# Four stores issued by ScalarE in y steps 4 and 5 in place of SyncE in step 3, a load put behind the y products, and eight operand tiles moved by 32 words

## The chip, the core and the metric

One core of a Trainium2 chip. A kernel is timed in device microseconds for one execution; the kernel before took 1453.03 us (median of 3 runs, 1451.39 to 1453.51).

Engines: PE is TensorE (matmuls; PEld is its loading of the stationary operand), DVE VectorE, ACT ScalarE, POOL GpSimd, SP SyncE. Each works through its own instructions in the order of the program. SP issues the kernel's DMAs; SPq in the profile is its instruction queue. Engines wait for each other, and for DMAs, by semaphores.

## What is computed

Two layers, each of a Fourier mixing block A and a shift MLP block B, on x of 2048 rows by 512:

```python
def _A_ref(x, dft_seq_re, dft_seq_im, dft_hid_re, dft_hid_im):
    a = jnp.einsum("bsd,ed->bse", x, dft_hid_re)
    b = jnp.einsum("bsd,ed->bse", x, dft_hid_im)
    y = jnp.einsum("ts,bse->bte", dft_seq_re, a) - jnp.einsum("ts,bse->bte", dft_seq_im, b)
    return y

x = x + _A_ref(_layernorm(x))
x = x + _B_ref(_layernorm(x))      # B: layernorm, w1, gelu, shifts by 1 and 2 rows, w2, layernorm, w3, gelu, w4
x = x + _A_ref(_layernorm(x))
x = x + _B_ref(_layernorm(x))
```

Block A takes nearly all that is spoken of here. Block B begins with z, the normed result of A, in turned form (features on the partitions).

## The kernel before

**Products.** Every fp32 number is split in a high and a low part of the type fp32r, and a product is three matmuls (`mm3`, lines 307 to 309): high by high, high by low, low by high. Each matmul has a stationary operand of 128x128 and a moving operand of 128x512. `mm_half` makes two such products, six matmuls.

**Block A by chunks.** The 2048 rows of the result are four chunks c of 512. For each chunk `x_phase` runs eight steps k with the stationary operands `ax[k]`, then `y_phase` eight steps k with `ay[k]`; the moving operand of both is a piece of the sequence matrix, which comes from HBM (`in_ws`). The first chunk of layer 0 has `plain_phase` in place of both. So there are seven x phases and seven y phases. A y step has two items, "by1" and "by0", each of 12 matmuls; `y_order` gives the items in the order 0 by1, 0 by0, 1 by1, ... 5 by0, 6 by1, 7 by1, 6 by0, 7 by0. They are counted 0 to 15 here: items 8 and 9 are step 4, items 10 and 11 step 5, item 12 is 6 by1 and item 13 is 7 by1. An x step has 18 matmuls. After the last chunk's y phase, four "hid" products (96 matmuls, tiles `ring`, `rr`) multiply by the hidden matrix (`in_hs`), and then block B starts (`by_pairs`) with `zt[0]`, the first chunk's turned z, as a moving operand.

**How a moving operand is made.** Each y step needs two pieces of 512 KB. SP loads them into two of four buffers `raw0` to `raw3` (line 235): even steps use raw0 and raw1, odd steps raw2 and raw3. For each item DVE subtracts the pieces (line 259: `ring0f<-raw`), ACT casts the difference to the high part (line 260), DVE makes the low part (line 270: `ring<-ring0f`). There are four `ring` slots; item n uses slot n modulo 4. `stream` works three items ahead on line 259 and two items ahead on line 270, so DVE's order in a y phase is: line 259 of item n+1, line 270 of item n, line 259 of item n+2, line 270 of item n+1, and so on. A load into a raw buffer waits until DVE has done line 259 of both items that read it.

**The turned z of the first chunk.** In the last chunk's y phase (c = 3) `hook(k)` runs other work at the head of each step's by1 item. In steps 1 and 2 ACT norms the four z tiles of the first chunk (line 661); in steps 2 and 3 DVE turns them into `turn0` (line 605, two in each step). In step 3 `turn_out` stores `turn0` to HBM as four DMAs of 256 KB (line 615, buffer `zd`), and in step 6 `turn_in` loads it back as one DMA of 1 MB into `zt[0]` (line 620, `zt0f`), which lies where `ay[0]` and `ay[1]` were. Both are issued by SP, in one line with the loads of line 235. ACT splits `zt0f` and DVE makes its low part (lines 435 and 438) during the hid products.

**Where the operands lie.** All tiles lie in one arena per partition and are placed by a word number (a word is 4 bytes). `ay[0]` to `ay[3]` lie at words 0, 2048, 24640 and 26688. `ZW` is 4128, the length of `zt[0]`; `ay[4]` to `ay[7]` follow each other from there, each 2048 words, then `ax[0]` and `ax[1]`. `ax[2]` to `ax[7]` lie from word 15424. 2048 and 1536, the lengths of an `ay` and an `ax`, are multiples of 64 words (256 bytes), and so are 24640 and 15424; 4128 is 64 times 64 and 32 over.

Of the kernel before, what the change touches and what calls it, by code (L numbers as in the profile page):

```python
# [13 lines left out]
P = 128  # L14
S, D, F = 2048, 512, 1376
# [3 lines left out]
NP = NT // 2  # L19
# [4 lines left out]
DH = D // 2  # L24
NF = -(-F // P)
B = 32
NB = P // B
# [3 lines left out]
HALO = 2  # L31
# [13 lines left out]
def spectral_mlp_kernel(ctx: ExitStack, tc: tile.TileContext, x, ws, hs, w1, w2, w34, out, out_t):  # L45
    nc = tc.nc
# [30 lines left out]
    ZW = KD * 2 * SW  # L77
    AX, AY = 3 * 2 * DH, 4 * 2 * DH
    W12, XS = 2 * ZW, 2 * ZW + 8 * 2 * CH
    H3 = XS + NT * D  # L80
# [9 lines left out]
    def at(name, word, *shape, dtype=F32R):  # L90
        return nc.alloc_sbuf_tensor_at(name, [P, *shape], dtype, offset=base + 4 * word).ap()

    def both(name, word, *shape):
        return at(name, word, *shape), at(name + "f", word, *shape, dtype=F32)

    ay_at = [0, AY, H3, H3 + AY] + [ZW + (k - 4) * AY for k in range(4, NP)]
    ay, ayf = zip(*(both(f"ay{k}", word, 4, 2, DH) for k, word in enumerate(ay_at)))
    ax, axf = zip(
        *(both(f"ax{k}", ZW + 4 * AY + k * AX if k < 2 else XS - 2 * D + (k - 2) * AX, 3, 2, DH) for k in range(NP))
    )  # L100
    zt, ztf = zip(*(both(f"zt{i}", i * ZW, KD, 2, SW) for i in range(2)))
    w12 = [at(f"w12{i}", W12 + i * 4 * CH, 2, 2, CH) for i in range(4)]
# [3 lines left out]
    turn0 = at("turn0", EXT, KD, CH, dtype=F32)  # L106
# [42 lines left out]
    def xt(j):  # L149
        return xs[j // 2][:, j % 2]  # L150
# [4 lines left out]
    count = {"mm": 0, "tmp": 0, "turn": 0}  # L155
# [68 lines left out]
    def rows(sb, d, j, n, load):  # L224
        v = d[j * P : (j + n) * P, :].rearrange("(t p) d -> p t d", p=P)
        nc.sync.dma_start(*((sb, v) if load else (v, sb)))
# [127 lines left out]
    def normed_act(o, s, mr):  # L354
        nc.scalar.activation(o, s, AF.Identity, bias=mr[2], scale=mr[1])
# [84 lines left out]
    late = {}  # L440

    def plain_phase(hook):

        for k in range(NP):
            first, last = k == 0, k == NP - 1
            a = {"11": ay[k][:, 2], "22": ay[k][:, 3], "21": mid[k % 4][:, 0], "12": mid[k % 4][:, 1]}
            s = stream()
            hook(2 * k)
            jobs = ((PB, a["21"], s[:, 1]), (PA, a["11"], s[:, 1]), (PC, a["12"], s[:, 0]), (PD, a["22"], s[:, 0]))
            if first:  # L450
                mm_first(jobs[:2])
                mm_first(jobs[2:])
            else:
                for job in jobs:
                    mm_half(*job, False, False)
            s = stream()
            hook(2 * k + 1)
            mm_half(PC, a["11"], s[:, 1], False, last)
            mm_half(PD, a["21"], s[:, 1], False, last)
            mm_half(PB, a["22"], s[:, 0], False, last)  # L460
            mm_half(PA, a["12"], s[:, 0], False, last)
# [17 lines left out]
    def run_late(*names):  # L479
        for i in names:  # L480
            for f in late.pop(i, ()):
                f()
# [120 lines left out]
    def turn_one(t, q, u):  # L603
        v = t.rearrange("p d (a q j) -> p d a q j", a=NB, q=TC)[:, :, :, q]
        nc.vector.transpose(v, blocks_of(u))

    def turn_out(t, to=None):

        if to is None:
            count["turn"] += 1  # L610
            to = zd[count["turn"] % 2]
        z = to.rearrange("(e i) t -> i e t", i=B)
        for b in range(NB):
            v = t[b * B : (b + 1) * B].rearrange("i d (a t) -> i (d a) t", a=NB)
            nc.sync.dma_start(z[:, :, b * P : (b + 1) * P], v)  # L615

    def turn_in(dst, col):

        z = zd[count["turn"] % 2].rearrange("(d p) t -> p d t", p=P)
        nc.sync.dma_start(dst[:, :, 1, col : col + CH], z)  # L620
# [183 lines left out]
    def by_pairs(layer, zs, xin, dst):  # L804
# [3 lines left out]
        for q in range(TC):  # L808
            turn_one(turn2, q, zs[4 + q])
        turn_out(turn2)  # L810
        state["limit"] += 2
        w2p = [stream(), stream()]
# [154 lines left out]
        A(5, norm(10, 11))  # L967
        D(7, turn(sc0, 2, 2, 3))
        A(7, lambda: turn_out(sc0))
        A(9, lambda: turn_in(ztf[0], HALO))  # L970
        A(12, z_highs(0))
# [13 lines left out]
        D(14, turn(sc1, 3, 0, 1))  # L985
        D(15, turn(sc1, 3, 2, 3))
        A(15, lambda: turn_out(sc1), lambda: edges(NC - 1), lambda: left_halo(3))
        A(17, lambda: turn_in(ztf[1], HALO))
        A(21, z_highs(3))
# [547 lines left out]
    for layer in range(LAYERS):  # L1537
# [4 lines left out]
        for c in range(NC):  # L1542
            if layer == 0 and c == 0:
# [58 lines left out]
                def hook(i):  # L1602
                    k, odd = divmod(i, 2)
                    state["limit"] = w_items[layer]
                    if not odd:
                        if k + 1 < NP:
                            xp_norm(k + 1, 3)
                            xp_main(k + 1)
                        if not k:
                            xp_main_lows(1)  # L1610
                    else:
                        if 0 < k < NP - 1:
                            xp_main_lows(k + 1)
                        if k + 2 < NP:
                            xp_stats(k + 2)
                        if k:
                            xp_sums(k - 1)
                            xp_highs(k - 1, False)
                            xp_lows(k - 1, False)
# [32 lines left out]
            def hook(k):  # L1652
                if k == 1 and c:
                    rows(X1, x1d, (c - 1) * TC + 2, 2, False)
                if c == NC - 1:
                    if k == 6:
                        rows(xs[2], x1d, 4, 2, True)
                    if k in (1, 2):
                        for j in (2 * k - 2, 2 * k - 1):
                            zs[j] = tmp[:, j]  # L1660
                            normed_act(zs[j], xt(j), ln2[j])
                    if k in (2, 3):
                        for j in (2 * k - 4, 2 * k - 3):
                            turn_one(turn0, j, zs.pop(j))
                    if k == 3:
                        turn_out(turn0)
                    if k == 6:
                        turn_in(ztf[0], HALO)

            y_phase(c, hook)  # L1670

        tmps[:] = singles
        count["tmp"] = 0
        run_late("im1-")
        run_late("re1+")
        for i, (ri, dp) in enumerate(HORDER):
# [81 lines left out]
```

## Time and profile before

| | us |
|---|---|
| median of 3 runs | 1453.03 |
| the profiled execution's own time | 1454.25 |
| its span, from the first to the last instruction | 1452.3 |
| PE busy | 1433.5 (99%) |
| DVE busy | 1148.7 (79%) |
| ACT busy | 727.1 (50%) |
| mean granted TensorE clock | 0.994 of full |

The span is what the trace covers; the time of an execution holds another 1.95 us around it. A row of the timeline or the chain begins with its start and its length in us; a busy PE is not PE at its peak, since the ends of matmuls are modelled: how fast PE goes is read from the distance between the starts of matmuls.

### The profile page before, as it was taken

How to read it: one execution, taken by the hardware profiler on the slowest of the kernel's cores; microseconds unless marked ns; L12 is line 12 of the kernel's file. 1: busy time of each engine (PE TensorE's matmuls, PEld its weight loads, DVE VectorE, ACT ScalarE, POOL GpSimd, SP SyncE). 2: the span in 40 equal slices, each digit the busy share in tenths (PEclk: the TensorE clock that was granted, in tenths of full speed). 3: DMA queues.
4: the chain of work that ended last, by engine and by line, in shares of the span. 5: the costliest groups of instructions: out<-in, count | busy, mean ns of one | idle time of the engine just before them, and what ended most of it. 6: DMA issues, size and time to landing. Idle time of an engine off the chain costs nothing.

```text
span 1452.3 us, 17275 instructions
## 1 busy us (share of the span) xinstructions
PE 1433.5 (99%) x6258; PEld 1177.6 (81%) x6258; DVE 1148.7 (79%) x1602; ACT 727.1 (50%) x979; POOL 78.7 (5%) x111
## 2 busy tenths in 40 slices
PE   9999999999799999999999999999998999999998
PEld 7888888888688888888888888888886888888887
DVE  7876987987778888667899879879887698637585
ACT  5553454455366755435554544544454666424352
POOL 2100000000001000000000000000000010000000
PEclk9999999999899999999999999999999999999999
DMA  7326655657554858959756466574666559656594
GB/s 248 129 88 203 203 181 194 205 164 261 196 155 119 284 201 311 380 206 340 237 170 203 159 194 209 163 228 166 198 220 220 157 125 338 196 192 248 171 312 148
DMA packets 136813, 302.13 MB, mean 208 GB/s; under 512 B 15372, under 2 KB 61196, under 8 KB 133528
## 3 DMA queue, kind: packets, MB, share of 16 engines
q1 hardware_dynamic: 136728, 301.03, 62.6%
q8 instruction: 49, 0.80, 0.2%
q14 instruction: 36, 0.29, 0.1%
HBM read 246.18 MB, written 54.81 MB: 207 GB/s over the span
## 4 chain that ended last, share of the span: by engine, by line
PE 93%; DVE 4%; DMA 2%; SPq 1%; issue 0%; ACT 0%; POOL 0%; DVEq 0%; ACTq 0%; POOLq 0%
PE psd L307 10%; PE psd L309 10%; PE psd L308 10%; PE psa L307 8%; PE psa L309 8%; PE psa L308 8%; PE psb L308 6%; PE psc L308 6%; PE psc L307 6%; PE psc L309 6%; PE psb L309 6%; PE psb L307 6%; DMA raw<-in_ws 2%; DVE ring L270 1%; SPq L615 0%
## 5 line engine op out<-in xcount | busy, mean ns | idle before, releaser
L253 ACT CAST ring<-raw 128x1024 fp32r<-128x1024 f32 x127 | 133.2, 1052 | 107.8 <-PE psd L309 50.9
L270 DVE TENSOR_TENSOR ring<-raw,ring 128x1024 fp32r<-128x1024 f32 (+1 forms) x128 | 154.6, 1211 | 24.2 <-ACT ring L253 24.1
L307 PE MATMUL psd<-ring,rr 128*128 128x512 f32 x208 | 81.0, 389 | 0.0
L309 PE MATMUL psd<-ring,rr 128*128 128x512 f32 x208 | 81.0, 389 | 0.0
L308 PE MATMUL psd<-ring,rr 128*128 128x512 f32 x208 | 80.9, 389 | 0.0
L260 ACT CAST ring<-ring0f 128x1024 fp32r<-128x1024 f32 x28 | 29.5, 1054 | 70.1 <-DVE ring0f L259 70.1
L308 PE MATMUL psb<-ring,ay 128*128 128x512 f32 x128 | 51.5, 402 | 13.0 <-DVE ring L270 13.0
L347 POOL TENSOR_TENSOR rs<-ve,mhalf 128x4 f32<-128x4 f32 x16 | 28.7, 1795 | 615.5 <-DVE nm L346 615.5
L270 DVE TENSOR_TENSOR ring<-ring1f,ring 128x512 fp32r<-128x512 f32 (+1 forms) x56 | 53.2, 950 | 0.8 <-ACT ring L256 0.8
L309 PE MATMUL psb<-ring,ay 128*128 128x512 f32 x128 | 51.1, 400 | 0.0
L326 POOL TENSOR_TENSOR rs<-ve,mhalf 128x2 f32<-128x2 f32 (+1 forms) x33 | 29.3, 887 | 397.0 <-DVE nb L325 397.0
L307 PE MATMUL psb<-ring,ay 128*128 128x512 f32 x128 | 50.6, 396 | 0.0
L307 PE MATMUL psc<-ring,ay 128*128 128x512 f32 x128 | 50.5, 394 | 0.0
L308 PE MATMUL psc<-ring,ay 128*128 128x512 f32 x128 | 50.4, 394 | 0.0
L307 PE MATMUL psa<-ring,ay 128*128 128x512 f32 x126 | 50.3, 399 | 0.0
L309 PE MATMUL psc<-ring,ay 128*128 128x512 f32 x128 | 50.1, 391 | 0.0
L309 PE MATMUL psa<-ring,ay 128*128 128x512 f32 x126 | 50.1, 397 | 0.0
L308 PE MATMUL psa<-ring,ay 128*128 128x512 f32 x126 | 50.0, 397 | 0.0
L308 PE MATMUL psd<-ring,ay 128*128 128x512 f32 x126 | 49.4, 392 | 0.0
L309 PE MATMUL psd<-ring,ay 128*128 128x512 f32 x126 | 49.4, 392 | 0.0
L307 PE MATMUL psd<-ring,ay 128*128 128x512 f32 x126 | 49.4, 392 | 0.0
L260 ACT CAST ring<-ring1f 128x1024 fp32r<-128x1024 f32 x28 | 29.5, 1055 | 36.9 <-DVE ring1f L259 36.9
(566 smaller groups left out, 4381.0 us busy)
## 6 DMA issues: line engine op xcount, KB each, us to landing
raw<-in_ws SPq DMA_DIRECT2D x183, 512.0 KB, 4.9
raw<-in_hs SPq DMA_DIRECT2D x56, 512.0 KB, 3.6
w3b<-w3d SPq DMA_DIRECT2D x15, 1792.0 KB, 8.6
w4r<-w4a SPq DMA_DIRECT2D x33, 512.0 KB, 6.4
wq<-w4a SPq DMA_DIRECT2D x22, 512.0 KB, 4.9
w3d<-w3b SPq DMA_DIRECT2D x5, 1792.0 KB, 6.7
x1d<-tmp SPq DMA_DIRECT2D x12, 512.0 KB, 5.9
xs<-x1d SPq DMA_DIRECT2D x12, 512.0 KB, 5.1
```

The costliest lines, as they stand in the source:

```text
L253: nc.scalar.copy(dest[:, a:b, 0], r[0][:, a:b])
L260: nc.scalar.copy(dest[:, :, 0], lo)
L270: nc.vector.tensor_tensor(lo[:, i], src[:, i], hi[:, i].bitcast(F32), op=ALU.subtract)
L307: nc.tensor.matmul(o, lh, rh, start=first, stop=False, skip_group_check=onto)
L308: nc.tensor.matmul(o, lh, rl, start=False, stop=False, skip_group_check=onto)
L309: nc.tensor.matmul(o, ll, rh, start=False, stop=last, skip_group_check=onto)
L326: nc.gpsimd.tensor_tensor(rs[:, :n], ve[:, :n], mhalf[:, 0, :n], op=ALU.pow)
L347: nc.gpsimd.tensor_tensor(rs, ve, mhalf[:, :, :2], op=ALU.pow)
```

## The change

```diff
-    ay_at = [0, AY, H3, H3 + AY] + [ZW + (k - 4) * AY for k in range(4, NP)]
+    ay_at = [0, AY, H3, H3 + AY] + [ZW + B + (k - 4) * AY for k in range(4, NP)]
...
-        *(both(f"ax{k}", ZW + 4 * AY + k * AX if k < 2 else XS - 2 * D + (k - 2) * AX, 3, 2, DH) for k in range(NP))
+        *(both(f"ax{k}", ZW + B + 4 * AY + k * AX if k < 2 else XS - 2 * D + (k - 2) * AX, 3, 2, DH) for k in range(NP))
...
-    def turn_out(t, to=None):
+    def turn_out(t, to=None, queue=nc.sync, which=range(NB)):
...
-        for b in range(NB):
+        for b in which:
...
-            nc.sync.dma_start(z[:, :, b * P : (b + 1) * P], v)
+            queue.dma_start(z[:, :, b * P : (b + 1) * P], v)
...
-                    if k == 3:
-                        turn_out(turn0)
-                    if k == 6:
-                        turn_in(ztf[0], HALO)
+                    if k in (4, 5):
+                        turn_out(turn0, queue=nc.scalar, which=range(2 * k - 8, 2 * k - 6))
...
         tmps[:] = singles
         count["tmp"] = 0
+        turn_in(ztf[0], HALO)
         run_late("im1-")
```

`B` is 32 words. `ay[4]` to `ay[7]`, `ax[0]` and `ax[1]` move from word 4128 to word 4160, which is 65 times 64; `ax[1]` then ends where `ax[2]` begins. The four stores are issued by ACT, two at the head of step 4 and two at the head of step 5, and the load of `zt0f` is issued by SP after the y phase. No other DMA moves to another engine. Both layers have the same differences.

On SP, in the last chunk's y phase, the rows around the four stores (raw buffers with their numbers; the first two loads are those of step 5, the last two those of step 6):

```order
 L235 DMA raw2_178<-in_ws 128x1024
 L235 DMA raw3_179<-in_ws 128x1024
-L615 DMA zd1_80<-turn0_150 32x16x128 x4
 L235 DMA raw0_176<-in_ws 128x1024
 L235 DMA raw1_177<-in_ws 128x1024
```

The loads of step 6 stand directly behind those of step 5, with nothing between that waits for the turning.

On SP further on, at the end of the y phase (`in_hs` is the hidden matrix, `in_w1` and `in_w2` weights of block B, `xs` a part of x):

```order
 L235 DMA raw1_177<-in_hs 128x1024
 L226 DMA xs2_143<-x1d_78 128x2x512
-L620 DMA zt0f_133<-zd1_80 128x4x512
 L235 DMA raw2_178<-in_hs 128x1024
 L235 DMA raw3_179<-in_hs 128x1024
 L235 DMA raw0_176<-in_w1 128x1024
 L235 DMA raw1_177<-in_w1 128x1024
+L620 DMA zt0f_133<-zd1_80 128x4x512
 L235 DMA raw2_178<-in_w2 128x1024
```

The load of `zt0f` moves behind two loads of the hidden matrix and two of the weights.

On ACT, in the same y phase, the casts of items 10 to 15 (ring2, ring3 are items 10 and 11, ring0 and ring1 items 12 and 13, then 14 and 15):

```order
 L260 CAST ring2_172<-ring2f_173 128x2x512
 L260 CAST ring3_174<-ring3f_175 128x2x512
-L260 CAST ring0_168<-ring0f_169 128x2x512
-L260 CAST ring1_170<-ring1f_171 128x2x512
+L615 DMA zd1_80<-turn0_150 32x16x128 x2
+L260 CAST ring0_168<-ring0f_169 128x2x512
+L260 CAST ring1_170<-ring1f_171 128x2x512
+L615 DMA zd1_80<-turn0_150 32x16x128 x2
 L260 CAST ring2_172<-ring2f_173 128x2x512
 L260 CAST ring3_174<-ring3f_175 128x2x512
```

Two issues now stand between the casts of items 11 and 12, and two between those of items 13 and 14.

More of the change, by code (lines that the diff above doesn't have):

```diff
@@ L605, in turn_one @@
         nc.vector.transpose(v, blocks_of(u))
-    def turn_out(t, to=None):
+    def turn_out(t, to=None, queue=nc.sync, which=range(NB)):
         if to is None:
-            count["turn"] += 1
+            count["turn"] += which[0] == 0
             to = zd[count["turn"] % 2]
         z = to.rearrange("(e i) t -> i e t", i=B)
-        for b in range(NB):
+        for b in which:
             v = t[b * B : (b + 1) * B].rearrange("i d (a t) -> i (d a) t", a=NB)
-            nc.sync.dma_start(z[:, :, b * P : (b + 1) * P], v)
+            queue.dma_start(z[:, :, b * P : (b + 1) * P], v)
     def turn_in(dst, col):
```

## The prediction

> **What bounds the kernel now.** First the page's chain that ended last, by engine:
>
> ```profile
> PE 93%; DVE 4%; DMA 2%; SPq 1%; issue 0%; ACT 0%; POOL 0%; DVEq 0%; ACTq 0%; POOLq 0%
> ```
>
> PE sets the end. There is something to win only where PE waits or where its matmuls stand further apart. So next the view of waits, for PE alone (us in total, times, longest):
>
> ```profile
> PE psb L308 <- DVE ring L270: 13.0, 2, 7.4
> ```
>
> This is the first row and PE's only long wait, once in each layer. The chain of waits in layer 0 tells how it comes about:
>
> ```profile
> 368.27 1.23 DVE turn L605 x2
> 369.51 0.33 SPq L615
> 369.88 1.44 SPq L615
> ...
> 372.93 1.50 SPq L235
> ...
> 374.47 8.09 DMA raw<-in_ws
> ...
> 382.69 1.23 DVE ring0f L259
> 383.91 1.14 DVE ring L270
> ```
>
> SP stands at the first store until DVE has turned the last two tiles (369.49), issues four stores, and only then, at 372.93, the loads of step 6. These land behind the stores, 8.09 us after the chain's piece begins. DVE waits at line 259 of item 12 until 382.69, and the low part of item 11, which is queued behind it on DVE, ends at 385.05. PE needs that at the second matmul of item 11.
>
> **What the wait costs.** The windows view (stretch, its length, PE busy, PEld, DVE, ACT, POOL, granted clock, DMA share, GB/s) of the wait and of what follows it, layer 0 and then layer 1, and PE's timeline at the ends of both:
>
> ```profile
> 377.53:385.10 7.57, 0.17 (x2) 0.00 (x1) 2.36 (x2) 1.04 (x1) 0.00 (x0) 0.69 0.62 226
> 385.10:390.74 5.64, 5.64 (x13) 4.43 (x14) 5.17 (x5) 2.10 (x2) 0.00 (x0) 0.51 0.13 23
> 1103.50:1107.48 3.98, 3.98 (x10) 3.13 (x10) 3.82 (x4) 1.29 (x2) 0.00 (x0) 0.51 0.00 0
> ```
>
> ```profile
> 377.30 0.40 PE L307 MATMUL psb<-ring,ay 128*128 128x512 f32 x1
> 390.74 0.39 PE L309 MATMUL psc<-ring,ay 128*128 128x512 f32 x1
> 1097.52 0.40 PE L307 MATMUL psb<-ring,ay 128*128 128x512 f32 x1
> 1107.48 0.39 PE L308 MATMUL psa<-ring,ay 128*128 128x512 f32 x1
> ```
>
> After the wait PE runs at a granted clock of 0.51 for 5.6 and 4.0 us. From 377.30 to 390.74 are 14 distances; at the 0.2325 us that they have around here (next part) they would take 3.26, so 13.44 - 3.26 = 10.2 us are lost. In layer 1, 10 distances: 9.96 - 2.33 = 7.6. Together **17.8 us**.
>
> **The moved operands.** PE's timeline at the first matmuls of y steps 3, 4 and 5, then of x steps 0 and 2 of another chunk with the two products between them, then of the plain phase's step 4 and its end:
>
> ```profile
> 363.49 0.39 PE L307 MATMUL psc<-ring,ay 128*128 128x512 f32 x1
> 368.93 0.40 PE L307 MATMUL psc<-ring,ay 128*128 128x512 f32 x1
> 374.51 0.40 PE L307 MATMUL psc<-ring,ay 128*128 128x512 f32 x1
> 193.87 0.39 PE L307 MATMUL psc<-ring,ax 128*128 128x512 f32 x1
> 202.24 0.39 PE L307 MATMUL psd<-ring,rr 128*128 128x512 f32 x1
> 204.96 0.39 PE L307 MATMUL psc<-ring,ax 128*128 128x512 f32 x1
> 50.83 0.39 PE L307 MATMUL psb<-ring,rr 128*128 128x512 f32 x1
> 95.19 0.40 PE L307 MATMUL psc<-ring,ax 128*128 128x512 f32 x1
> ```
>
> Step 3 takes 5.44 us for 24 matmuls (0.2267 each), step 4 takes 5.58 (0.2325). Both are unstalled and of one shape; `ay[3]` lies on a multiple of 64 words, `ay[4]` 32 over. x steps 0 and 1 take 8.37 for 36 (0.2325), though they come at the start of a phase; the 12 products with `rr`, which lies on such a multiple, take 2.72 (0.2267). So the distance goes with the address, not with the place in a phase. Moved to word 4160, these six tiles should give 0.2267. Seven y phases have 4 x 24 = 96 such matmuls, seven x phases 36: 924 x 0.0058 = 5.4 us. Steps 4 to 7 of the plain phase, where every second product has another operand, take 44.36 for 192 against 192 x 0.2267 = 43.52: 0.8. Together **6.2 us**, all on PE and so on the path.
>
> The Trainium skill, "TensorE: Matmul & The Clock Gate", section LDWEIGHTS, gives a weight load by its columns alone, 128/1.2 = 107 ns by its formula, and knows no address; by it the load is hidden, this term would be 0 and the sum 6.2 us smaller. The trace does not agree that all spacings of one shape are equal; why they differ no run here shows yet.
>
> **What is late next.** With the stores gone from SP, four things remain to be followed in the last y phase. DVE's and ACT's rows there, and two of the chunk before (c = 2), where nothing is stored:
>
> ```profile
> 365.92 1.22 DVE L259 TENSOR_TENSOR ring1f<-raw,raw 128x1024 f32<-128x1024 f32 x1
> 371.64 1.21 DVE L259 TENSOR_TENSOR ring3f<-raw,raw 128x1024 f32<-128x1024 f32 x1
> 373.92 1.21 DVE L477 TENSOR_TENSOR rr00f<-rr00f,rr11f 128x1024 f32<-128x1024 f32 x1
> 372.94 1.06 ACT L260 CAST ring<-ring3f 128x1024 fp32r<-128x1024 f32 x1 [1.22 <-DVE ring3f L259]
> 270.45 1.22 DVE L259 TENSOR_TENSOR ring3f<-raw,raw 128x1024 f32<-128x1024 f32 x1
> 277.06 1.23 DVE L259 TENSOR_TENSOR ring1f<-raw,raw 128x1024 f32<-128x1024 f32 x1 [0.85 <-DMA raw<-in_ws]
> ```
>
> One DVE operation follows another after 1.14 us.
>
> *Step 6's loads* can go when item 9's line 259 is done: 365.92 + 1.14 = 367.1. With the 6.1 us to landing of the DMA rows below they are there by 373.6, and DVE comes to item 12 at 373.92 + 1.14 = 375.1. Item 11's low part is then done at 375.1 + 2 x 1.14 = 377.3; PE, 36 faster matmuls into the slow steps, wants it at 377.53 - 0.2 = 377.3. The wait is gone, with no room to spare.
>
> *Step 7's loads* go at 371.64 + 1.14 = 372.8. In c = 2 the same loads, issued at 270.45 + 1.14 = 271.6, let DVE go on at 277.06, 5.4 us later; before the change, beside four stores, step 6's loads took from 372.93 to 382.69, 9.7. Now two stores, issued by ACT from 374.0 (372.94 + 1.06), come 1.2 us behind them: half of the stores, and behind in place of ahead, so I take a quarter of the difference, 6.5 us: DVE does item 13's line 259 at 379.3 and item 12's low part is ready at 379.3 + 2.28 = 381.6. PE wants it at 377.3 + 12 x 0.2267 + 0.1 = 380.1. **A wait of 1.5 us**; with the ends 5.4 and 9.7 it is 0.4 and 4.7.
>
> ```profile
> 766.60 0.39 PE L307 MATMUL psc<-ring,ax 128*128 128x512 f32 x1
> 767.07 0.50 PE L308 MATMUL psc<-ring,ax 128*128 128x512 f32 x1
> 767.41 0.39 PE L309 MATMUL psc<-ring,ax 128*128 128x512 f32 x1
> raw<-in_ws SPq DMA_DIRECT2D x12, 512.0 KB, 6.1
> zd<-turn SPq DMA_DIRECT2D x4, 256.0 KB, 3.9
> ```
>
> Whether so short a wait lowers the clock the trace doesn't show. After the 0.47 us from 766.60 to 767.07 the next distance is 0.34, and no slow row follows. After layer 1's wait it costs 1.9 (3.98 us for 9 distances in place of 2.09). I take 0, the nearer row, and keep 1.9.
>
> *ACT's issues.* SP's issues of these stores took 0.33 to 1.44 us, the first of a pair the shorter; two are some 1.8. The first pair holds ACT from 374.0 to 375.8, before item 12's cast can start (376.2). The second follows item 13's cast (about 381.5), and delays item 14's to 383.3; DVE takes up item 14's low part five operations after 379.3, at 385.0. So 0. That cover is gone from some 1.5 us an issue on: then item 14 comes after PE, 2 us later for each us more.
>
> *The hid products.* Their first needs a chain: item 13 from PSUM (line 527), a cast, three DVE operations, the last of which is line 438:
>
> ```profile
> 393.97 1.39 DVE L527 SCALAR_TENSOR_TENSOR rr10f<-psc,rr11f 128x512 f32<-128x512 f32 x2 [0.15 <-PE psc L309]
> 398.75 1.22 DVE L438 TENSOR_TENSOR rr<-rr10f,rr 128x1024 fp32r<-128x1024 f32 x1
> 401.47 0.40 PE L307 MATMUL psc<-ring,rr 128*128 128x512 f32 x1
> 408.04 1.05 ACT L435 CAST zt<-zt0f 128x1024 fp32r<-128x1024 f32 x1
> 423.27 0.40 PE L307 MATMUL psd<-zt,w 128*128 128x512 f32 x1
> ```
>
> It takes 398.75 + 1.14 - 393.97 = 5.9 us and had 2.0 us to spare (third matmul at 401.93). Now DVE comes to it seven operations after 379.3, at 387.3, and ends it at 393.2. PE, from 381.35 on with 48 matmuls, is there at 392.2 and wants the low part at 392.7: **0.5 us of wait**. The hidden matrix's loads, in one line with the second pair of stores, could make it 0 to 5.
>
> *The load of `zt0f`* goes 0.4 us before the hid products' start in place of 11.4 us before, since it stands behind the second weight load (issued when DVE is done with a piece of the hidden matrix). Landed 6 to 8 us later it holds the cast at 408.04, 6.6 us after that start, by 1 or 2 us, and block B's first matmul is 21.8 us after the start. So 0; were it split only some 20 us after the start, each us more would be one of PE.
>
> **The sum.** 17.8 + 6.2 - 2 x (1.5 + 0.5) = 20.0. Layer 1 has the same order of instructions, so its new waits count the same. From the profiled execution, 1454.25 - 20.0 = 1434.3; that execution is 1.2 above the median, so against it 1433.0. I say **1434**.
>
> **The rivals.**
>
> *The stores still collide* (0.20). Step 7's loads take 9.7 us as step 6's did: per layer a wait of 4.7, a lower clock for 1.9, and 0.5: 14.2 in all, a gain of 9.8, 1443. For it: 7.6 of the 9.7 us were spent at a DMA share of 0.62 and 226 GB/s, so the loads were slowed by something other than bytes. Against it: fewer stores, later ones. The Trainium skill, "DMA: Bandwidth & Descriptors", section Issuing engines are not separate DMA queues, says that DMAs of all engines run on the same 16 DMA engines and interleave, and that issuing from another engine saves only its issue time; by that rule the move to ACT frees SP and nothing more, and this rival is what it makes of step 7. The trace of before, where SP issues all, cannot show it.
>
> *The address does nothing* (0.10), as part of the change not doing what it says: 0.2325 stays, because it is of the step and not of the place. Then 17.8 - 4.0 = 13.8: 1440. Against it speak x steps 0 and 1.
>
> *The wait only moves* (0.04): with no room at item 11 (377.3 against 377.3) and step 7's loads also late, all of the 17.8 returns and 6.2 may not show: 1447 to 1453.
>
> *ACT is held by its stores* (0.04; slower). Were an issue on ACT to hold it until the store has landed (T), item 12's low part would come at 374.0 + 2T + 1.05 + 1.14, item 14's at 378.3 + 4T: waits of 2T - 3.9 and 2T - 3.3, and both lower the clock (3.8). At T = 3.9, the landing above, that is 12.2 a layer, and 1453.0 - 24.0 + 24.4 = 1453.4; at 4.5, a little above it, 1458. It is slower than before from T = 3.9 on. Against it: on SP an issue took at most 1.44 while its store landed in 3.9.
>
> **How the numbers follow.** Forecast 0.62, with 1430 (no wait left) to 1438 (the clock drops at both waits); collision 0.20, address 0.10, moved 0.04, held 0.04. 1429 to 1444 leaves out the last two, the worse half of the collision and little below: under 2 in 10. A measurement of this kernel can tell some 0.2%, 2.9 us, from no change. Faster by more: all but the last two and a little, 0.94; within: 0.03; slower: 0.03.
>
> **What would show it.** In the trace after: SP's step 6 loads issued some 2 us before the turning ends in place of 3.4 behind it; no wait of PE at item 11; 96 matmuls of y steps 4 to 7 in 21.8 us in place of 22.3, x steps 0 and 1 in 8.16; a wait of 0.4 to 2 us at item 12 for item 13's loads, and up to 1 at the first hid product, at full clock. The forecast is wrong if PE waits at line 308 by over 4 us again, if ACT's row before item 12's cast is idle beyond 376.5, or if block B's first matmul waits for `zt`.

## The result, and the profile after

| | us |
|---|---|
| kernel before, median of 4 runs | 1453.27 (1451.39 to 1455.76) |
| changed kernel, median of 4 runs | 1437.59 (1437.10 to 1437.62) |
| ratio, 95% interval | 0.989, 0.9873 to 0.9907 |
| profiled execution before, after | 1454.25, 1437.62 |
| its span before, after | 1452.3, 1435.6 |

The change makes the kernel 1.1% faster. One execution of the kernel before, beside four of the experiments, fell in a slower state (1589.12 us at a mean clock of 0.849) and is in no median. The two profiled executions lie 16.6 us apart; the forecast had 20.0. The chain that ended last, by engine, and PE's waits (us in total, times, longest) in the kernel after:

```profile
PE 89%; DVE 6%; DMA 3%; issue 1%; ACT 0%; SPq 0%; POOL 0%; DVEq 0%; ACTq 0%; POOLq 0%
```

```profile
PE psc L308 <- DVE ring L270: 3.4, 2, 1.7
PE psd L162 <- POOL mhalf L58: 1.4, 1, 1.4
PE psc L309 <- DVE rr L438: 0.9, 4, 0.2
PE psb L307 <- DMA w3b<-w3d: 0.8, 1, 0.8
PE psd L307 <- DMA w4u<-w4s: 0.2, 1, 0.2
```

The 13.0 us at item 11 (product `psb`) are gone. The largest wait now is at item 12 (`psc`), once a layer; the second row is the start of the kernel. The chain gives DVE 6% of the span, some 86 us, while PE's waits hold 7 us in all: where DVE and PE hand over to each other closely, the chain is followed back along DVE. So what is lost is read from the waits, not from these shares.

PE's timeline at the four places where it waits in layer 0 (item 12, the two hid places, block B), and the windows view (stretch, length, PE busy, PEld, DVE, ACT, POOL, granted clock, DMA share, GB/s) of the stretch behind the first of them:

```profile
377.42 0.39 PE L307 MATMUL psc<-ring,ay 128*128 128x512 f32 x1
379.52 0.50 PE L308 MATMUL psc<-ring,ay 128*128 128x512 f32 x1 [1.72 <-DVE ring L270]
379.86 0.40 PE L309 MATMUL psc<-ring,ay 128*128 128x512 f32 x1
...
390.54 0.39 PE L308 MATMUL psc<-ring,rr 128*128 128x512 f32 x1
391.14 0.50 PE L309 MATMUL psc<-ring,rr 128*128 128x512 f32 x1 [0.21 <-DVE rr L438]
...
396.48 0.39 PE L308 MATMUL psc<-ring,rr 128*128 128x512 f32 x1
397.08 0.50 PE L309 MATMUL psc<-ring,rr 128*128 128x512 f32 x1 [0.21 <-DVE rr L438]
...
657.50 0.39 PE L309 MATMUL psc<-b,w3b 128*128 128x512 f32 x1
658.70 0.50 PE L307 MATMUL psb<-b,w3b 128*128 128x512 f32 x1 [0.81 <-DMA w3b<-w3d]
```

```profile
379.52:385.10 5.58, 5.58 (x25) 4.62 (x26) 5.55 (x5) 2.26 (x3) 0.00 (x0) 1.00 0.95 277
```

A wait costs more than the number in brackets: the distance of two starts less 0.23, and 0.11 more in the distance behind it (0.34). At item 12 that is 2.10 - 0.23 + 0.11 = 1.98 us, at each of the two hid places 0.60 - 0.23 + 0.11 = 0.48, at block B's 1.08. The clock behind item 12's wait is full, 25 matmuls in 5.58 us; before it was 0.51.

DVE, ACT and SP in the same part of the kernel after:

```profile
368.98 1.21 DVE L259 TENSOR_TENSOR ring3f<-raw,raw 128x1024 f32<-128x1024 f32 x1
373.52 1.22 DVE L270 TENSOR_TENSOR ring<-ring3f,ring 128x1024 fp32r<-128x1024 f32 x1
377.11 1.23 DVE L259 TENSOR_TENSOR ring1f<-raw,raw 128x1024 f32<-128x1024 f32 x1 [2.37 <-DMA raw<-in_ws]
370.28 1.06 ACT L260 CAST ring<-ring3f 128x1024 fp32r<-128x1024 f32 x1 [1.22 <-DVE ring3f L259]
370.30 0.89 ACTq L615 DMA_DIRECT2D zd<-turn  x2
370.22 0.80 SPq L235 DMA_DIRECT2D raw<-in_ws  x2
```

Step 7's loads can go when line 259 of item 11 is done, at 368.98 + 1.14 = 370.1; DVE waits for them until 377.11, 7.0 us. ACT's sequencer (ACTq) issues the first two stores at 370.30, 0.02 us after the cast ahead of them has begun, not after it has ended. So they start together with step 7's loads, which SP issues from 370.22 on; what that costs the loads, a run below shows.

Where the gain went, by the distances of PE's starts in both traces:

| | forecast, us | in the traces, us |
|---|---|---|
| long wait at item 11 and half clock behind it | 17.8 | 17.8, of which 0.4 stays as small distances |
| moved operands | 6.2 | 6.2 |
| waits at item 12, both layers | -3.0 | -3.9 (1.98 and 1.91) |
| waits at the hid products | -1.0 | -1.9 (four of 0.48) |
| waits of block B for DMAs | 0 | -1.6 (1.08 at 657.50, 0.5 at 1386.13) |
| sum | 20.0 | 16.2; 0.4 of the 16.6 is in rows not followed |

### The profile page after: what moved, and what is told of

Same layout as the page of the kernel before. It is cut to its first block, busy times and chain, and to the rows that moved or that the text cites. A ratio compares the mean times of both kernels' runs of the same rounds, so it can differ in the third digit from the quotient of the medians.

```text
span 1435.6 us, 17273 instructions
## 1 busy us (share of the span) xinstructions
PE 1424.8 (99%) x6258; PEld 1173.5 (82%) x6258; DVE 1147.9 (80%) x1602; ACT 726.6 (51%) x979; POOL 78.6 (5%) x111
## 4 chain that ended last, share of the span: by engine, by line
PE 89%; DVE 6%; DMA 3%; issue 1%; ACT 0%; SPq 0%; POOL 0%; DVEq 0%; ACTq 0%; POOLq 0%
PE psd L307 10%; PE psd L309 10%; PE psd L308 10%; PE psa L307 8%; PE psa L308 8%; PE psa L309 8%; PE psc L309 6%; PE psc L308 6%; PE psc L307 6%; PE psb L307 6%; PE psb L309 6%; PE psb L308 6%; DVE ring L270 2%; DMA raw<-in_ws 2%; DMA w3b<-w3d 1%
## 5 line engine op out<-in xcount | busy, mean ns | idle before, releaser
L308 PE MATMUL psb<-ring,ay 128*128 128x512 f32 x128 | 50.1, 392 | 0.0
L309 PE MATMUL psb<-ring,ay 128*128 128x512 f32 x128 | 49.8, 389 | 0.0
L307 PE MATMUL psb<-ring,ay 128*128 128x512 f32 x128 | 49.8, 389 | 0.0
L307 PE MATMUL psa<-ring,ay 128*128 128x512 f32 x126 | 49.0, 389 | 0.0
L308 PE MATMUL psa<-ring,ay 128*128 128x512 f32 x126 | 49.0, 389 | 0.0
L309 PE MATMUL psa<-ring,ay 128*128 128x512 f32 x126 | 49.0, 389 | 0.0
```

Of the source, the lines that this page charges most:

```text
L307: nc.tensor.matmul(o, lh, rh, start=first, stop=False, skip_group_check=onto)
L308: nc.tensor.matmul(o, lh, rl, start=False, stop=False, skip_group_check=onto)
L309: nc.tensor.matmul(o, ll, rh, start=False, stop=last, skip_group_check=onto)
```

## The experiments

Ten kernels. Their ratios are against the kernel before on the same chip: its median was 1453.96 us for the shift alone, the stores alone, everything 32 words on and the doubled turns, 1452.97 for the last four below, and one run of 1454.67 stood beside the four distances and the moved `ring`.

**The shift alone.** The changed kernel's places of operands, the stores and the load as before.

```diff
-                    if k in (4, 5):
-                        turn_out(turn0, queue=nc.scalar, which=range(2 * k - 8, 2 * k - 6))
+                    if k == 3:
+                        turn_out(turn0)
+                    if k == 6:
+                        turn_in(ztf[0], HALO)
```

> The kernel before with nothing but the six operand tiles moved by 32 words. Theory (a stationary operand that starts 32 words past a multiple of 64 costs 5.8 ns a matmul): 924 x 0.0058 + 0.8 = 6.2 us less than before, some 1447.0, with the long wait still there in both layers; y steps 4 to 7 in 21.8 us in place of 22.3 where nothing waits. Rival (the spacing belongs to the steps, or came with the stores): within 1 us of before.

Measured: 1446.48 us (1446.08 to 1447.71), ratio 0.9952 (0.9936 to 0.9967). PE's first row of waits:

```profile
PE psb L308 <- DVE ring L270: 11.9, 2, 6.2
```

The long waits stay, a little shorter (11.9 us in place of 13.0), and still 7.5 us are won; y step 4 of chunk c = 1 takes 5.44 us (170.38 to 175.82). The shift has a worth of its own that needs no help from the stores.

**The stores and the load alone.** The operands back at word `ZW`.

```diff
-    ay_at = [0, AY, H3, H3 + AY] + [ZW + B + (k - 4) * AY for k in range(4, NP)]
+    ay_at = [0, AY, H3, H3 + AY] + [ZW + (k - 4) * AY for k in range(4, NP)]
...
-        *(both(f"ax{k}", ZW + B + 4 * AY + k * AX if k < 2 else XS - 2 * D + (k - 2) * AX, 3, 2, DH) for k in range(NP))
+        *(both(f"ax{k}", ZW + 4 * AY + k * AX if k < 2 else XS - 2 * D + (k - 2) * AX, 3, 2, DH) for k in range(NP))
```

> The changed kernel with the six tiles back at their old words, so only the stores and the load are moved. Theory (the two parts add up): the changed kernel's 1437.6 and 6.2 us, 1443.8, perhaps 0.4 less, since a slower PE comes later to item 12 and waits there some 1.6 in place of 1.87 us. Rival (the shift did something for the waits too): 1446 or more, with a wait at item 12 of 3 us or more.

Measured: 1442.69 us (1441.41 to 1443.64), ratio 0.9924 (0.9908 to 0.9939). The two ratios multiply to 0.9876; the kernel with both has 0.989 (0.9873 to 0.9907). Within these intervals the parts add up. PE waits 1.7 us at item 12, as with the shift, not the 3 of the rival.

**Everything 32 words on.** The arena's base is moved, so that every tile of the arena changes its address and none its distance to another (one buffer of a small pool makes the room).

```diff
-    base = -(-nc.sbuf_base // 32) * 32
+    base = -(-nc.sbuf_base // 32) * 32 + 4 * B
```

> The changed kernel with the whole arena 32 words further on (and one buffer less of each small statistics tile to make room), so that nearly every stationary operand, some 6200, starts 32 words past a multiple of 64. Theory (it is the address of the stationary operand alone): all distances of 0.2267 us become 0.2325, some 6200 x 0.0058 = 36 us more, 1470 to 1476; the products with zt as the moving operand keep theirs or take as much more. If the moving operand's address counts as well and adds up: some 70 us more. Rival (it is something of those tiles' neighbourhood or of those steps): within 2 us of the changed kernel.

Measured, one run: 1439.66 us. PE's starts of y steps 4 and 5 and the end of step 5, chunk c = 1:

```profile
170.54 0.39 PE L307 MATMUL psc<-ring,ay 128*128 128x512 f32 x1
175.98 0.39 PE L307 MATMUL psc<-ring,ay 128*128 128x512 f32 x1
181.42 0.39 PE L307 MATMUL psc<-ring,ay 128*128 128x512 f32 x1
```

Steps of 5.44 us, 0.2267 a matmul, as in every other y step. Nothing got slower: the address of the weights by itself is not it, and the theory that the forecast gave for its 6.2 us falls. The 2 us above the changed kernel are another thing. Here is PE at item 12, and the windows behind it:

```profile
377.64 0.39 PE L307 MATMUL psc<-ring,ay 128*128 128x512 f32 x1
380.15 0.57 PE L308 MATMUL psc<-ring,ay 128*128 128x512 f32 x1 [2.13 <-DVE ring L270]
```

```profile
380.15:384.00 3.85, 3.85 (x10) 3.03 (x11) 3.85 (x4) 1.45 (x2) 0.00 (x0) 0.56 0.84 218
```

The wait is 0.4 us longer than in the changed kernel, and 10 matmuls behind it run at a clock of 0.56. Why the loads came 0.4 us later here isn't settled.

**The weights at four distances.** Next theory: what counts is where the weights lie against the moving operand `ring`, modulo 64 words. `ay[4]` to `ay[7]` are put 32, 24, 16 and 8 words short of ring's place.

```diff
-    ay_at = [0, AY, H3, H3 + AY] + [ZW + B + (k - 4) * AY for k in range(4, NP)]
+    ay_at = [0, AY, H3, H3 + AY] + [ZW + (k - 4) * (AY + 8) for k in range(4, NP)]
```

> The changed kernel with y's four moved operands 0, 8, 16 and 24 words behind their place in the kernel before: ay4, ay5, ay6, ay7 now lie 32, 24, 16 and 8 words short of the place (mod 64 words) at which ring lies. A run with everything 32 words on slowed nothing, so not the address alone counts. Theory (what counts is where the weights lie against the moving operand, mod 64 words, and any difference costs the whole): all four steps at 0.2325 us a matmul, 4 x 7 x 24 x 0.0058 = 3.9 us, 1441.5. Rival A (only the half of 64 words that is read together counts): ay4 0.2325, and ay5 to ay7 in proportion, 0.2311, 0.2296, 0.2282: 2.4 us, 1440.1. Rival B (only a distance of exactly 32 costs): ay4 alone, 1.0 us, 1438.6. Read from the spacing in each of y steps 4 to 7.

Measured, one run: 1440.14 us. Starts of y steps 3, 4 and 5 of chunk c = 1, of items 12 to 15 (6 by1, 7 by1, 6 by0, 7 by0), and of the x phase behind them:

```profile
165.57 0.39 PE L307 MATMUL psc<-ring,ay 128*128 128x512 f32 x1
171.02 0.40 PE L307 MATMUL psc<-ring,ay 128*128 128x512 f32 x1
176.60 0.39 PE L307 MATMUL psc<-ring,ay 128*128 128x512 f32 x1
182.21 0.40 PE L307 MATMUL psc<-ring,ay 128*128 128x512 f32 x1
184.97 0.40 PE L307 MATMUL psc<-ring,ay 128*128 128x512 f32 x1
187.76 0.39 PE L307 MATMUL psb<-ring,ay 128*128 128x512 f32 x1
190.51 0.39 PE L307 MATMUL psb<-ring,ay 128*128 128x512 f32 x1
193.31 0.39 PE L307 MATMUL psc<-ring,ax 128*128 128x512 f32 x1
```

Step 3, at distance 0, takes 5.45; steps 4 and 5, at 32 and 24 words, take 5.58 and 5.61, that is 0.2325 and 0.2338 a matmul. Steps 6 and 7 alternate by items of 12 matmuls: at 16 words an item takes 2.76 and 2.75 (0.2296), at 8 words 2.79 and 2.80 (0.2329). So 8, 24 and 32 words cost the whole, as the theory has it, and 16 words about half of it, as rival A has it for that one distance; why, no run shows. The total is that of rival A, but by accident: the spacing adds 0.53 us a phase, 3.7 in seven, and block B's waits of the changed kernel (1.6) were absent in this execution.

**The moving operand moved instead.** The weights at their old place, and `ring` with what lies behind it 32 words on.

```diff
-    RNG = RR + 2 * KD * 2 * CH
+    RNG = RR + 2 * KD * 2 * CH + B
...
-    ay_at = [0, AY, H3, H3 + AY] + [ZW + B + (k - 4) * AY for k in range(4, NP)]
+    ay_at = [0, AY, H3, H3 + AY] + [ZW + (k - 4) * AY for k in range(4, NP)]
```

(`ax[0]` and `ax[1]` too are back at `ZW`; one buffer of a small pool outside the arena makes the room.)

> The stores as in the changed kernel; ay4 to ay7, ax0 and ax1 back at their old place, and in their stead ring, the moving operand, 32 words further (and what lies behind it). Theory (the place of the weights against the moving operand counts): y steps 4 to 7 and x steps 0 and 1 at 0.2267, y steps 0 to 3, x steps 2 to 7 and the products of ring and rr slow at 0.2325. Rival (the weights' own address counts): as in the kernel before, y steps 0 to 3 fast and 4 to 7 slow. The time by the theory: y phases as in the kernel with the stores alone (1442.7), x phases 7 x 72 x 0.0058 = 2.9 more, products with rr some 2 more: about 1447.5; by the rival 1442.7.

Measured, one run: 1459.57 us. Starts of y steps 2 to 6 of chunk c = 1:

```profile
162.94 0.40 PE L307 MATMUL psc<-ring,ay 128*128 128x512 f32 x1
168.53 0.39 PE L307 MATMUL psc<-ring,ay 128*128 128x512 f32 x1
174.10 0.39 PE L307 MATMUL psc<-ring,ay 128*128 128x512 f32 x1
179.54 0.39 PE L307 MATMUL psc<-ring,ay 128*128 128x512 f32 x1
184.98 0.39 PE L307 MATMUL psc<-ring,ay 128*128 128x512 f32 x1
```

Now steps 2 and 3 take 5.59 and 5.57, and steps 4 and 5, with the very addresses that were slow in the kernel before, 5.44. The distance between the two operands is shown as the cause. The total is 12 us above the expectation. Matmul for matmul against the trace of the kernel with the stores alone, the spacing loses 3.0 us in the x phases, as expected, but 5.0 in the products of `ring` and `rr`, where 2 were counted, and 8.0 in block B, which was forgotten: there one operand often lies behind `ring` and the other not, and the spacing is 0.231 to 0.234 as well. Behind item 12's waits of 2.0 us the clock also fell (last section).

**More work ahead of item 11.** The two turns of step 3 are made twice.

```diff
-                            turn_one(turn0, j, zs.pop(j))
+                            u = zs.pop(j)
+                            for _ in range(k - 1):
+                                turn_one(turn0, j, u)
```

> The changed kernel with the two turns of step 3 made twice, 1.22 us more of DVE in each layer ahead of step 7's loads. Theory (DVE has no room left in the last y phase, so what comes on it there lands on PE): PE's waits at items 11 and 12 together grow by 1.0 to 1.3 us a layer, 1439.6 to 1440.2. Rival (only the collision of the first two stores with step 7's loads makes the wait at item 12, and DVE has room): 1437.6 within 0.5.

Measured: 1439.73 us (1438.99 to 1440.48), ratio 0.9903 (0.9886 to 0.9921). PE's waits:

```profile
PE psc L308 <- DVE ring L270: 3.6, 3, 1.7
PE psb L308 <- DVE ring L270: 2.7, 2, 1.5
```

The second row is item 11, back with 1.2 and 1.5 us, about as much as the two further turns take on DVE. So "no room to spare" was right: what is added on DVE ahead of item 11 went straight to PE.

**Issued by SP at the same places.**

```diff
-                        turn_out(turn0, queue=nc.scalar, which=range(2 * k - 8, 2 * k - 6))
+                        turn_out(turn0, which=range(2 * k - 8, 2 * k - 6))
```

> The changed kernel with the four stores at the same places of the program, but issued by SP. The first pair then stands on SP ahead of step 7's loads, the second ahead of those of y step 0 of the next part. Theory (the place in time counts, not the issuer): the trace of after shows ACT's stores starting at 370.30, with step 7's loads (370.1), so it is the same whether SP or ACT issues them: item 12's wait 1.7 us plus the two issues on SP ahead of the loads (0.3 to 1.5 us), 1437.6 to 1440. Rival (ACT as issuer is what helps, as SP's order holds the loads behind the stores): step 7's loads land 3 us later, waits of 4.7 us at half clock, about 1446.

Measured: 1435.87 us (1435.46 to 1436.37), ratio 0.9883 (0.9867 to 0.9900), 1.7 us below the expected range. SP's rows and DVE at item 13:

```profile
366.86 0.86 SPq L615 DMA_DIRECT2D zd<-turn  x2
370.24 0.83 SPq L235 DMA_DIRECT2D raw<-in_ws  x2
```

```profile
376.49 1.22 DVE L259 TENSOR_TENSOR ring1f<-raw,raw 128x1024 f32<-128x1024 f32 x1 [1.74 <-DMA raw<-in_ws]
```

SP issues the first pair 3.4 us earlier than ACT does, since it has no cast of item 11 ahead of it, and step 7's loads are there after 376.49 - 370.1 = 6.4 us in place of 7.0; item 12 waits 1.1 us. So it isn't the issuer that helps but the place in the program, behind the loads of step 6. The Trainium skill, "DMA: Bandwidth & Descriptors", section Issuing engines are not separate DMA queues, says that DMAs of all engines run on the same 16 DMA engines and interleave. The traces agree: step 7's loads, issued by SP, land later beside stores of either issuer (6.4 and 7.0 us) than beside none (5.5 us, two runs further on).

**The load back in step 6.**

```diff
                         turn_out(turn0, queue=nc.scalar, which=range(2 * k - 8, 2 * k - 6))
+                    if k == 6:
+                        turn_in(ztf[0], HALO)
...
-        turn_in(ztf[0], HALO)
         run_late("im1-")
```

> The changed kernel with the load of zt0f back in y step 6. Theory: the load is nowhere on the path (block B's first matmul waits for nothing in the trace of after, 21 us behind the hid products' start), and back in step 6 it lies beside loads that have room: 1437.6, within 0.5. Rival (it was moved because it delays the loads of the hidden matrix): the waits at the hid products, 0.21 us each in after, grow to 1 to 2 us, 1440.

Measured: 1440.20 us (1438.85 to 1441.80), ratio 0.9912 (0.9898 to 0.9927). The theory falls, the rival stands. PE's waits, and ACT ahead of the hid products in layer 1:

```profile
PE psb L307 <- ACT beside L541: 3.0, 2, 2.3
```

```profile
1103.72 1.04 ACT L253 CAST ring<-raw 128x1024 fp32r<-128x1024 f32 x1 [3.56 <-DMA raw<-in_hs]
1104.67 1.07 ACT L541 COPY beside<-psb 128x512 f32<-128x512 f32 x2
```

The 1 MB of `zt0f` stands ahead of the hidden matrix's last two pieces; ACT waits 3.56 us for them, its copies out of PSUM are queued behind that cast, and PE waits 2.3 us for a bank that they free. Moving the load is worth some 2.6 us, by medians from two chips. In the kernel before, with this load at the same place, PE waits at none of the hid products; that the wait at item 11 gave the loads their time there is likely, but no run shows it.

**The stores one step later.**

```diff
-                    if k in (4, 5):
-                        turn_out(turn0, queue=nc.scalar, which=range(2 * k - 8, 2 * k - 6))
+                    if k in (5, 6):
+                        turn_out(turn0, queue=nc.scalar, which=range(2 * k - 10, 2 * k - 8))
```

> The changed kernel with the four stores one y step later on ACT, in steps 5 and 6. Theory (item 12 waits since the first pair of stores lies beside step 7's loads): these land 5.4 us after their issue at 370.1, as in chunk c=2, by 375.5, and item 12's wait falls from 1.72 and 1.64 us to 0.1 to 0.3: some 3 us less, 1434.2 to 1435; the stores then lie beside the hidden matrix's loads, and if those are delayed as step 7's were (1.6 us), the hid products take back up to 3.2 in all. Rival (the loads take 7 us with or without the stores, because of what else DVE does ahead of item 13): the wait stays 1.7, 1437.6.

Measured: 1434.05 us (1433.30 to 1435.57), ratio 0.9871 (0.9856 to 0.9886). DVE at item 13 and PE's waits:

```profile
375.49 1.23 DVE L259 TENSOR_TENSOR ring1f<-raw,raw 128x1024 f32<-128x1024 f32 x1 [0.93 <-DMA raw<-in_ws]
```

```profile
PE psc L309 <- DVE rr L438: 0.8, 4, 0.2
PE psc L308 <- DVE ring L270: 0.6, 2, 0.4
```

With no store beside them step 7's loads, issued from 370.04 on, land 5.5 us after their issue, as in chunk c = 2, and item 12 waits 0.2 and 0.4 us in place of 1.7. The hidden matrix's loads, now beside the stores, have the room: the hid waits are unchanged. So the first pair of stores was item 12's wait.

**And the second pair of turns behind item 12's operations.** The run before, with the turns of step 3 done in step 4 between two items (and the stores in steps 5 and 6).

```diff
-                    if k in (2, 3):
-                        for j in (2 * k - 4, 2 * k - 3):
+                    if k == 2:
+                        for j in (0, 1):
                             turn_one(turn0, j, zs.pop(j))
+                    if k == 4:
+                        late["y4"] = [lambda j=j: turn_one(turn0, j, zs.pop(j)) for j in (2, 3)]
...
+                if k == 4:
+                    run_late("y4")
```

> As the run before (stores in steps 5 and 6), and the second pair of turns moved on DVE from step 3 to step 4, between the operations of items 12 and 13. Theory (DVE has no room ahead of items 11 and 12, so two turns of 1.14 us there cost what they delay): item 11's and item 12's operations come 2.3 us earlier, step 6's and 7's loads too, and the waits at items 11 and 12 are 0; the turns now delay what follows by 2.3, which meets the hid products' chain: at most as large as after's there (0.9 in all). Sum 1433 to 1434.5, the fastest of the set. Rival (the room is missing later as well): hid products wait 2.3 a layer more, 1437 to 1439.

Measured: 1432.92 us (1432.31 to 1434.09), ratio 0.9863 (0.9848 to 0.9877). PE's waits:

```profile
PE psc L309 <- DVE rr L438: 1.0, 4, 0.4
PE psb L307 <- DMA w3b<-w3d: 0.9, 1, 0.9
```

No wait is left at items 11 and 12. The median is 1.1 us below that of the run before, which still waited 0.6 us there; the ranges of the two overlap, so that step by itself isn't shown. (A turn takes 0.6 us, not the 1.14 of the expectation.) Of all the kernels this has the lowest ratio, 0.9863 against the changed kernel's 0.989; the two intervals just overlap. Its median is 4.7 us lower, on a chip where the kernel before was 0.3 lower too.

## Why the prediction came out as it did

The forecast of 1434 was 3.6 us below the median of 1437.59, inside the range and on the right side, and no rival came. The mechanism held, with three waits sized too small; one term was right in size by luck.

*The long wait and its clock* (17.8) went as forecast. Item 11's distances are together 0.1 and 0.3 us over the usual in the two layers, and doubling the turns brings the wait back at once.

*The moved operands* (6.2; six tiles, `ay[4]` to `ay[7]`, `ax[0]` and `ax[1]`, not the eight of the title) were right in size; the reason was not. The forecast put it on the address of the weights, a multiple of 64 words or not. Moving everything changed nothing; moving `ring` alone turned fast and slow steps around. It is the place of the weights against the moving operand. In the kernel before both readings name the same six tiles, so its trace could not tell them apart, and that the wrong one gave the right number was luck. The rival "the address does nothing" is excluded by the shift alone.

*Item 12's wait* (1.5 a layer, ends 0.4 and 4.7) measured 1.98 and 1.91. The step that was off: ACT's stores were to begin only when the cast ahead of them had ended, 1.2 us behind the loads, and a quarter of the spread of the landings was taken for that. In the trace ACT's sequencer did not wait for its own running cast (370.28 and 370.30); the stores came at the same time as the loads (370.22), and these took 7.0 us, not 6.5. That the stores set it at all is shown by the run with the stores one step later (5.5). The clock did not fall, as taken; three of the other runs show how near that was.

*The hid products* (0.5 a layer) wait 0.48 at the place that the forecast named, and as much again 5.9 us later, where the same kind of chain, a cast and line 438, ends once more 0.5 us late. The forecast followed only the first of them.

*Block B's waits* for weights (1.6 in all) were not in the sum. They are of the DMAs of `w3b` and `w4u`, hundreds of us behind the change. Two of the kernels with the stores on ACT (the doubled turns, and the stores one step later) have none in their traces, so they are not a cost of an edit by itself; what sets them stays open.

*ACT's issues* cost nothing, as taken: 0.3 to 0.5 us each, on a sequencer that is ahead of its engine. *The load of `zt0f` later* cost nothing, as taken. It went later still than forecast, 2.4 us behind the hid products' start (392.67 against 390.31), not 0.4 ahead of it; block B's first matmul did not wait all the same. But its other side was missed: left in step 6, it would have taken 2.6 us.

*"Stores still collide"*: the collision is real, a landing of 7.0 us beside two stores and of 5.5 beside none, and small against the 9.7 of before. Before, all four stood ahead of the loads in SP's queue; two that start beside them cost far less. What was said for this rival was misread: the window with a DMA share of 0.62, 377.53 to 385.10, begins 4.6 us behind the loads' start and reaches beyond their end. In the loads' own time, 372.93 to 382.69, the share was 0.87 at 255 GB/s; for step 7's loads in the run with the stores one step later, 370.04 to 375.49, it was 0.54 at 192.

## What to carry to other kernels

Where a wait goes, ask for each transfer of the stretch what will now meet it: the wait may also have been the time in which other loads landed. Put a store where no load is due next; moving it to another engine alone won nothing here. And on a kernel whose matmuls follow each other without a gap, measure the spacing for each pair of operands: here up to 3% was lost where the two operands of a matmul lay differently modulo 64 words.

## What the runs showed of the hardware

*Operand places.* A 128x128 by 128x512 fp32r matmul follows the one before it by 0.2267 us where weights and moving operand start at the same place modulo 64 words (256 bytes), by 0.2325 to 0.2338 at 8, 24 and 32 words of distance and by 0.2296 at 16; the address itself made no difference when all tiles of the arena moved together. Whether it is a matter of reading the two at one time no run shows.

*The clock after a wait.* In the twelve traces of this case, from 20 us on, there are 26 gaps of over 1 us between two starts of PE. After 17 gaps of 1.1 to 2.13 us no matmul was slow; after all 9 of 2.42 us and more, 7 to 12 were. Two gaps on either side of the border, the first from the kernel with the stores alone, the other from the one with `ring` moved, and the clock behind the latter:

```profile
380.10 0.39 PE L307 MATMUL psc<-ring,ay 128*128 128x512 f32 x1
382.23 0.50 PE L308 MATMUL psc<-ring,ay 128*128 128x512 f32 x1 [1.74 <-DVE ring L270]
```

```profile
384.27 0.39 PE L307 MATMUL psc<-ring,ay 128*128 128x512 f32 x1
386.69 0.50 PE L308 MATMUL psc<-ring,ay 128*128 128x512 f32 x1 [2.03 <-DVE ring L270]
```

```profile
386.70:391.00 4.30, 4.30 (x12) 3.37 (x13) 4.30 (x4) 1.91 (x2) 0.00 (x0) 0.60 0.86 242
```

So in this kernel a wait of 1.7 us costs itself, and one of 2.0 us costs 1.5 to 2 us more. The Trainium skill, "TensorE: Matmul & The Clock Gate", section What's actually happening, gives the half clock after at least one idle window of some 3.4 us; these runs show it after a wait of 2.0 us, so here the measurement decides; how the window counts, no run shows.

*A DMA issue on ACT* started 0.02 us after the start of the cast ahead of it in ACT's program (370.28 and 370.30, in the kernel after), that is while the cast ran. It must not be counted as behind it.
